# A recurrent attention kernel with a token-mixing layer: the written order of its instructions is replaced, and with it which engine copies, masks and sums

## The chip, the cores and the metric

One core of a Trainium2 chip runs the kernel. The time is device microseconds of one execution; a kernel's time is the median of its runs. The engines are TensorE (PE in the profile, its weight loads PEld), VectorE (DVE), ScalarE (ACT) and GpSimd (POOL); SyncE (SP) issues DMAs. GpSimd issues some DMAs too.

## What is computed

Six float32 inputs r, k, v, w, a, b of shape (4, 8, 768, 40) go through a recurrence over 768 steps for each of 4 batches and 8 heads, and its output, laid out as x of shape (4, 768, 320), goes through a mixing layer with four weight matrices. The output is float32 (4, 768, 320).

```python
for t in range(S):                       # state: (B, H, 40, 40)
    y[:, :, t] = einsum('bhd,bhde->bhe', rt, state)
    Sa = einsum('bhde,bhe->bhd', state, at)
    state_decay = state * wt[:, :, None, :] - einsum('bhd,bhe->bhde', Sa, bt)
    state = state_decay + einsum('bhd,bhe->bhde', vt, kt)
...
theta = x @ w_theta
zr = x * cos(theta)
zi = x * sin(theta)
y = w_tok_r @ zr + w_tok_i @ zi          # over the 768 tokens of a batch
u = x + y
out = u + maximum(u @ w_ch, 0)
```

## The kernel before, in words

Time is cut into chunks of 128 steps: 4 batches of 6 chunks make 24 tiles, numbered 0 to 23. A tile holds 128 steps of all 8 heads (128 partitions by 320 elements).

Within a tile the recurrence becomes matrix products. The logarithms of w (LN) are summed along the steps by two triangular products on TensorE: CSI, up to and with the step, and CSE, up to the step before, with five small products behind it for the decay over the whole tile. Exponentials of the sums (INVW, WI) scale k, b (KH, BH) and a (AH). The scaled inputs and r, v, cast to bf16 (CR, CV), are transposed on TensorE (TRK, TRA, TRR) and copied out of PSUM (EKBT, EAT, ERVT). Four sets of scores follow, each 8 products of 128 by 128: PSI and PHI (k and b against a), LV (v against r) and LU (the solved vectors nu against r). Each set fills two PSUM banks (tiles `sc`). Only entries above the diagonal count, so in the kernel before VectorE multiplies each set by a triangle of ones while it copies it to SBUF (`masked`, lines 374 to 379; EPSI, EPHI, ELV, ELU). Then X0, NU and NUT solve for nu, GT carries the state to the next tile (within a batch), GD transposes the state, and Y and EX give x.

The mixing layer works per tile too: XT, EXT, TH, ETH give theta; SIN gives cosine and sine of several tiles at once (`sines`, lines 483 to 489: three tiles together, for the last batch three, two and one); ZR and ZI multiply by x. YR sums twelve products (6 token blocks, real and imaginary) per tile, 24 tiles by 6 entries; EU adds x; UT, EUT, CH, EO, ST end the tile. The products need the two token matrices transposed: twelve row loads (LDT), twelve sets of transposes (WT) and copies (EWT).

The order of all this is written out by hand in the string `ORDER` (from line 19). An entry such as `EPSI:3V` names an operation, its tile, for some a part, its engine (A ScalarE, V VectorE, G GpSimd), and behind @ its PSUM tile (0 to 3 for the four one-bank tiles `sm`, 0 and 1 for the two-bank tiles `sc`). The loop at the end reads the entries one by one, so each engine runs its instructions in this order; the framework adds the waits for data and for buffers.

Loads are entries too: LDW, LDK, LDB, LDA, LDR, LDV load one input of one tile each (160 KB, `load`, line 282, on SyncE's queue; four buffers per input), ST stores from the same queue, LDT and LDC load matrices from GpSimd's queue (`row_load`, line 531). A load stands in line behind the loads ahead of it in the order.

Helpers record most instructions, so in the profile their lines stand for many operations: 259 is any product by `times`, 254 a copy on ScalarE, 256 a copy on another engine, 262 a product on TensorE, 266 a transpose, 525 the last step (EO), 487 a sine, 285 a load, 529 a store.

Of the kernel before, what the change touches and what calls it, by code (L numbers as in the profile page):

```python
# [19 lines left out]
LDK:0 LDW:1 LN:1A LDR:1 LDT:0.0G LDW:0 LN:0A LDC:0.2G LDB:0 LDC:0.0G LDA:0 LDV:1 LDW:2 CR:1A  # L20
LDR:0 LDT:1.0G CSE:1@0 LDV:0 LDC:0.3G LDW:3 WI:1A CSE:0@1 LDC:0.1G LDT:0.1G CSI:0@2 INVW:0A
LDA:1 WI:0A CSI:1@3 BH:0V LDB:3 KH:0V TRK:0@0 EKBT:0V INVW:1A CV:1A LDB:1 AH:0V TRA:0@2 EAT:0A
LDK:1 LN:2A PSI:0@0 PHI:0@1 EPSI:0V CSI:2@1 LDK:3 CR:0A EPHI:0V TRR:1@3 ERVT:1V CV:0A X0:0@0
LDK:2 ENX:0A LN:3A NU:0 LDR:2 TRR:0@2 ERVT:0A LV:1@0 LDB:2 CSE:2@3 LDA:2 ELV:1V AH:1V ENU:0A
INVW:2A LV:0@1 LDA:3 CSE:3@2 LDR:3 ELV:0V WI:3A TRA:1@0 EAT:1A GT:0@1 CSI:3@2 INVW:3A BH:1V
WI:2A LDV:2 KH:1V LDW:4 NUT:0@0 BH:3G EGT:0V TRK:1@2 EKBT:1V ENUT:0A LDV:3 KH:3G PSI:1@0 PHI:1@1
LDK:4 EPSI:1V KH:2G LDA:4 BH:2G X0:1@3 LDV:4 EPHI:1V AH:2G ENX:1A TRK:2@0 LU:0@0 TRA:2@1 LDR:4
EKBT:2V EAT:2A NU:1 LDR:5 CR:2G AH:3G TRK:3@2 ENU:1A PHI:2@1 GT:1@0 LDB:4 ELU:0V CV:2G EPHI:2V
EGT:1V NUT:1@1 CR:3G PSI:2@0 LDB:5 TRR:2@3 ENUT:1A LN:4A LDK:5 EPSI:2V ERVT:2A CV:3G TRA:3@1
EAT:3A LDW:5 LU:1@1 Y:0@0 X0:2@3 ENX:2A EKBT:3V LDW:6 CSE:4@1 LV:2@0 GD:0@2 EX:0V EGD:0A TRR:3@0  # L30
ELU:1V NU:2 CV:4G WI:4A LDW:7 CSI:4@2 INVW:4A PSI:3@1 AH:4G CR:4G LDA:5 Y:1@1 ENU:2A ERVT:3A
ELV:2V EPSI:3V NUT:2@2 PHI:3@0 KH:4G TRR:4@3 LDB:6 ENUT:2A ERVT:4A BH:4G LDK:6 GT:2@0 EX:1V
EPHI:3V LU:2@1 TRA:4@2 EGT:2V LDA:6 CR:5G EAT:4A XT:1@1 EXT:1A TRK:4@3 X0:3@2 LDV:5 ENX:3A LDV:6
TH:1@0 LN:5A ELU:2V LV:3@0 LDR:7 GD:1@1 NU:3 EKBT:4V ETH:1A ENU:3A CSI:5@3 INVW:5A ELV:3V LDV:7
PSI:4@1 BH:5G NUT:3@0 EGD:1A EPSI:4V GT:3@2 KH:5G XT:0@3 ENUT:3A LN:6A Y:2@1 LDK:7 CSE:5@0 LDR:6
EGT:3V EXT:0A PHI:4@0 WI:5A AH:5G EX:2V CSI:6@3 INVW:6A KH:6G X0:4@2 EPHI:4V LDB:7 LN:7A ENX:4A
LU:3@1 LDW:9 XT:2@0 EXT:2A TRK:5@1 CSE:6@3 ELU:3V NU:4 TH:2@0 WI:6A EKBT:5V ETH:2A BH:6G LV:4@0
ELV:4V TH:0@3 ENU:4A LDR:8 TRA:5@0 LDW:8 ETH:0A EAT:5A GD:2@1 CV:5G TRK:6@2 CV:7G PSI:5@1
NUT:4@3 EKBT:6V GT:4@0 LDA:8 EPSI:5V SIN:0.0A PHI:5@0 LDA:7 TRR:5@2 EGT:4V CV:6G AH:6G EGD:2V
X0:5@0 LDW:10 Y:3@1 ERVT:5V ENUT:4A ENX:5A EPHI:5V ZR:1G TRA:6@2 GD:3@3 EAT:6A LU:4@1 CR:7G  # L40
ZR:2G EX:3V EGD:3A NU:5 CR:6G CSE:7@1 ZR:0G ELU:4V LV:5@0 WI:7A LDB:9 CSI:7@2 INVW:7A LDB:8
LDV:10 TRR:6@3 LDR:10 ELV:5V ZI:1G LDK:8 PSI:6@1 BH:7G EPSI:6V Y:4@1 ENU:5A ERVT:6A PHI:6@0
LDK:9 LN:8A TRR:7@2 EX:4V X0:6@0 EPHI:6V ENX:6A LDR:9 NUT:5@3 ENUT:5A KH:7G TRK:7@1 EKBT:7V
LV:6@1 ERVT:7A CR:8G LDV:8 NU:6 ENU:6A GD:4@3 EGD:4A LDT:1.1G LU:5@0 CSI:8@1 AH:7G LDA:9 TRA:7@2
XT:3@0 ELV:6V NUT:6@3 EAT:7A ENUT:6A ELU:5V INVW:8A PSI:7@1 ZI:0G EXT:3V LN:9A GT:6@2 CSE:8@3
EPSI:7V TH:3@1 WI:8A LDR:11 Y:5@0 LN:10A AH:8G BH:8G LDV:9 EGT:6V XT:4@3 LDB:10 EX:5V PHI:7@0
ETH:3A LV:7@1 X0:7@1 EXT:4A EPHI:7V TRA:8@2 ENX:7A XT:5@3 TH:4@0 KH:8G EXT:5A LDW:12 EAT:8A
ZI:2G NU:7 LDK:10 TRK:8@3 CR:9G CR:10G ELV:7V CSI:9@2 ENU:7A INVW:9A BH:9G LU:6@0 TH:5@1 EKBT:8V
ETH:4A LDA:10 CSE:9@2 ETH:5A LDV:11 GT:7@3 ELU:6V CV:10G WI:9A LDB:12 PSI:8@1 EGT:7V Y:6@0
WT:0.0@1 EPSI:8V CV:8G NUT:7@2 LDW:11 PHI:8@0 WT:1.0@3 SIN:0.1A AH:9G EWT:0.0V TRR:8@1 ENUT:7V  # L50
LDT:2.0G EX:6V LDK:11 LU:7@1 EWT:1.0V EPHI:8V LDA:11 X0:8@2 ERVT:8A KH:9G WT:1.1@0 WT:0.1@3
ENX:8A EWT:0.1V CV:9G TRR:9@1 LDB:11 LV:8@0 ERVT:9A EWT:1.1V ZR:4G ZI:5G TRA:9@3 EAT:9A LDR:13
NU:8 LDV:14 ENU:8A LDA:12 ELV:8V TRK:9@0 XT:6@1 CSE:10@3 EKBT:9V GD:7@2 ZI:3G EXT:6V GD:6@0
ELU:7V ZR:3G CSI:10@1 INVW:10A LDT:4.0G PSI:9@0 LDV:12 EGD:7A EPSI:9V BH:10G EGD:6A PHI:9@1
LN:11A KH:10G GT:8@1 LDK:12 NUT:8@2 LDR:12 ENUT:8A EGT:8V EPHI:9V Y:7@0 X0:9@1 LDW:13 TH:6@2
WI:10A LU:8@0 ENX:9A EX:7V NU:9 ETH:6A ELU:8V LN:12A TRK:10@3 ENU:9A XT:7@2 LV:9@1 LDT:2.1G
AH:10G EXT:7A TRA:10@0 EKBT:10V ZI:4G Y:8@1 EAT:10A ELV:9V TH:7@2 ETH:7A ZR:5G LDK:13 GD:8@3
EGD:8A NUT:9@0 CR:11G EX:8V PSI:10@0 CV:11G GT:9@2 LDR:15 ENUT:9V CSI:11@3 INVW:11A EPSI:10V
XT:8@1 TRR:10@0 EXT:8A LDT:3.0G PHI:10@1 EGT:9V LDR:14 ERVT:10A CSE:11@3 WT:2.0@1 LDA:13
EPHI:10V LDV:13 KH:11G X0:10@2 WI:11A LDB:13 BH:11G ENX:10A TRR:11@0 LV:10@0 EWT:2.0V ERVT:11A  # L60
LU:9@1 AH:11G LDT:3.1G YR:0.0@3 ELV:10V NU:10 ENU:10A YR:0.1 TRK:11@1 ELU:9V LDW:14 TRA:11@0
LDT:5.0G LDT:4.1G YR:0.2 EAT:11A YR:0.3 YR:0.4 YR:0.5 EKBT:11V CSI:12@2 INVW:12A EU:0V TH:8@0
ETH:8A LN:13A PSI:11@0 EPSI:11V PHI:11@1 UT:0@1 CSE:12@2 CR:12G EUT:0A LDW:15 LDB:14 NUT:10@3
GT:10@0 ENUT:10A WI:12A EPHI:11V Y:9@1 CV:12G WT:3.0@3 KH:12G LV:11@0 AH:12G EGT:10V LU:10@1
EX:9V CR:15G WT:2.1@2 WT:3.1@0 SIN:1.0A YR:1.0@1 EWT:3.0V EWT:2.1V YR:1.1 BH:12G GD:9@3 EWT:3.1V
X0:11@2 YR:1.2 ELU:10V LDK:14 XT:9@0 YR:1.3 ENX:11A YR:1.4 EGD:9A ELV:11V NU:11 ENU:11A YR:1.5
ZI:8G EXT:9A TRA:12@3 TRK:12@2 Y:10@0 EU:1V EAT:12A EKBT:12V WT:4.0@3 LDT:5.1G NUT:11@1 ZR:6G
EX:10V CSI:13@2 INVW:13A KH:13G PSI:12@1 EWT:4.0V PHI:12@0 EPSI:12V ENUT:11A TRR:12@0 CH:0@3
EO:0V ERVT:12A ZR:7G GD:10@2 YR:2.0@1 YR:2.1 EGD:10A EPHI:12V ST:0 CSE:13@3 BH:13G X0:12@0
ENX:12A LU:11@1 LDA:14 WI:13A YR:2.2 ZI:6G ELU:11V UT:1@2 CR:13G LDR:17 LN:14A LV:12@0 EUT:1A  # L70
XT:10@3 CV:13G ELV:12V YR:2.3 NU:12 ENU:12A Y:11@2 EXT:10A AH:13G LDB:15 YR:2.4 LN:15A TRR:13@0
EX:11V TRA:13@3 ERVT:13V YR:2.5 EAT:13A ZI:7G CV:14G TRK:13@2 CR:14G EU:2V TH:9@0 EKBT:13V
GT:12@3 EGT:12V ETH:9A CH:1@1 PSI:13@1 PHI:13@0 EO:1V EPSI:13V ST:1 LDW:16 EPHI:13V CSI:14@2
INVW:14A KH:14G NUT:12@0 ENUT:12A CSE:14@3 WI:14A LDK:15 LDR:18 YR:3.0@1 TH:10@2 YR:3.1 LDA:16
X0:13@0 LDV:16 ETH:10A XT:11@3 EXT:11V LDA:15 CSI:15@2 ENX:13A LDB:16 AH:14G LV:13@1 LU:12@0
INVW:15A BH:14G TRA:14@3 NU:13 ENU:13A YR:3.2 ELV:13V ELU:12V YR:3.3 YR:3.4 YR:3.5 EU:3V EAT:14A
LDV:15 TH:11@2 ETH:11A KH:15G TRK:14@0 CSE:15@3 EKBT:14V LN:16A LDW:20 GT:13@2 EGT:13V WI:15A
WT:4.1@1 LDK:17 LDK:16 NUT:13@0 WT:5.1@3 EWT:4.1V ZR:8G WT:5.0@2 EWT:5.1V YR:4.0@1 LDW:17
SIN:1.1A EWT:5.0V PSI:14@1 PHI:14@0 LDV:17 AH:15G TRR:14@3 Y:12@2 EPSI:14V ENUT:13A EX:12V
ZR:11G BH:15G EPHI:14V YR:4.1 YR:4.2 YR:4.3 ERVT:14A YR:4.4 ZI:10G UT:2@2 EUT:2V YR:4.5 LU:13@1  # L80
X0:14@0 EU:4V ELU:13V GD:12@3 ENX:14A CH:2@2 EGD:12A EO:2V XT:12@1 EXT:12A CV:15G LV:14@0 ST:2
UT:3@3 NU:14 ZR:9G TRA:15@1 EUT:3A ENU:14A TRK:15@2 LDR:16 TH:12@3 EAT:15A ELV:14V EKBT:15V
CH:3@0 EO:3V LDA:18 ETH:12A ZI:9G TRR:15@1 CSI:16@3 INVW:16A ERVT:15V PSI:15@1 EPSI:15V ST:3
PHI:15@0 BH:16G ZR:10G YR:5.0@2 LDA:17 NUT:14@0 LDV:18 ENUT:14A CSE:16@1 YR:5.1 GT:14@3 GD:13@0
WI:16A Y:13@1 EPHI:15V KH:16G LN:17A LDW:21 CV:17G LDW:18 EGT:14V CR:18G LU:14@1 LV:15@0 EGD:13A
YR:5.2 LDK:19 EX:13V CR:17G X0:15@0 ELU:14V AH:16G YR:5.3 ENX:15A LDW:19 CV:16G YR:5.4 LDB:17
XT:13@3 EXT:13A YR:5.5 TRK:16@1 EU:5V LDR:19 NU:15 ENU:15A CSE:17@3 TH:13@2 EKBT:16V CR:16G
TRA:16@0 Y:14@1 ETH:13A ELV:15V LDB:20 ZI:11G EAT:16A LDV:19 TRR:16@2 EX:14V LDK:18 PSI:16@1
EPSI:16V WI:17A AH:17G PHI:16@0 LN:18A NUT:15@0 ENUT:15A CV:18G XT:14@3 YR:6.0@1 YR:6.1 EPHI:16V
EXT:14A YR:6.2 CR:19G ERVT:16A YR:6.3 TH:14@0 UT:4@3 LDA:20 LU:15@1 EUT:4V ELU:15V LV:16@0  # L90
CSI:17@2 GT:15@3 LDB:18 ETH:14A INVW:17A LN:19A CH:4@0 UT:5@2 YR:6.4 EGT:15V EUT:5A YR:6.5 EO:4V
# [541 lines left out]
```

## Time and profile before

| | us |
|---|---|
| median of 3 runs (lowest, highest) | 225.95 (224.32, 226.55) |
| the profiled execution, its own time | 228.5 |
| its span, first to last instruction | 226.7 |
| TensorE busy | 199.1 |
| VectorE busy | 189.4 |
| ScalarE busy | 150.9 |
| GpSimd busy | 118.1 |

The busy time of TensorE is that of its matrix products, whose ends are modelled; where products follow each other closely their spans overlap, so the rate is read from one start to the next. On the other engines too an instruction's span reaches a little over the start of the next. A timeline row gives the start, the span, the engine, the line, the operation with its tiles and shape, how many were merged, and in brackets how long the engine had been idle and what ended it. Row groups give the number, the sum and the mean.

### The profile page before, as it was taken

How to read it: one execution, taken by the hardware profiler on the slowest of the kernel's cores; microseconds unless marked ns; L12 is line 12 of the kernel's file. 1: busy time of each engine (PE TensorE's matmuls, PEld its weight loads, DVE VectorE, ACT ScalarE, POOL GpSimd, SP SyncE). 2: the span in 40 equal slices, each digit the busy share in tenths (PEclk: the TensorE clock that was granted, in tenths of full speed). 3: DMA queues.
4: the chain of work that ended last, by engine and by line, in shares of the span. 5: the costliest groups of instructions: out<-in, count | busy, mean ns of one | idle time of the engine just before them, and what ended most of it. 6: DMA issues, size and time to landing. Idle time of an engine off the chain costs nothing.

```text
span 226.7 us, 8000 instructions
## 1 busy us (share of the span) xinstructions
PE 199.1 (88%) x3344; PEld 158.1 (70%) x3344; DVE 189.4 (84%) x298; ACT 150.9 (67%) x293; POOL 118.1 (52%) x181
## 2 busy tenths in 40 slices
...
GB/s 104 195 192 184 156 181 136 166 176 168 143 181 160 166 189 164 188 151 190 104 159 156 195 157 161 186 172 181 159 162 32 4 61 1 61 42 48 29 90 87
DMA packets 155684, 30.81 MB, mean 136 GB/s; under 512 B 150400, under 2 KB 155648, under 8 KB 155648
## 3 DMA queue, kind: packets, MB, share of 16 engines
q1 hardware_dynamic: 153216, 27.54, 66.7%
q0 software_dynamic: 2432, 2.77, 7.9%
q8 instruction: 26, 0.43, 0.8%
q14 instruction: 10, 0.08, 0.1%
...
## 4 chain that ended last, share of the span: by engine, by line
PE 50%; issue 6%; DMA 5%; POOL 4%; DVE 4%; ACT 2%; POOLq 0%; DVEq 0%; ACTq 0%
PE sm L262 28%; PE sm L266 13%; PE sc L262 9%; DMA raw_w<-in_w_dram 5%; POOL kb L259 2%; DVE psi L259 1%; POOL rv L256 1%; ACT rvT L254 1%; POOL zi L259 1%; POOL zr L259 1%; DVE phi L259 1%; DVE lamv L259 0%; DVE lamu L259 0%; POOL ah L259 0%; DVE oo L525 0%
## 5 line engine op out<-in xcount | busy, mean ns | idle before, releaser
L259 POOL TENSOR_TENSOR kb<-raw_b,invW 128x320 bf16<-128x320 f32 x22 | 19.0, 863 | 33.2 <-DVE kb L259 20.1
L262 PE MATMUL sm<-zr,wtok_r 128*128 128x320 bf16 x120 | 34.2, 300 | 0.0
L262 PE MATMUL sm<-zi,wtok_i 128*128 128x320 bf16 x120 | 34.2, 299 | 0.0
L259 DVE TENSOR_TENSOR psi<-sc,mask_p 128x1024 bf16<-128x1024 f32 x24 | 29.2, 1219 | 3.4 <-PE sc L262 3.3
L259 DVE TENSOR_TENSOR lamu<-sc,mask_p 128x1024 bf16<-128x1024 f32 x24 | 29.2, 1218 | 1.4 <-PE sc L262 1.3
L259 DVE TENSOR_TENSOR lamv<-sc,mask_p 128x1024 bf16<-128x1024 f32 x24 | 29.2, 1217 | 1.4 <-PE sc L262 1.3
L259 POOL TENSOR_TENSOR ah<-raw_a,Wi 128x320 bf16<-128x320 f32 x22 | 19.0, 864 | 21.4 <-issue 8.7
L259 DVE TENSOR_TENSOR phi<-sc,mask_p 128x1024 bf16<-128x1024 f32 x24 | 29.2, 1216 | 0.9 <-PE sc L262 0.9
L259 POOL TENSOR_TENSOR zi<-cs,x 128x320 bf16<-128x320 f32 x24 | 19.0, 798 | 10.1 <-ACT cs L487 10.1
L259 POOL TENSOR_TENSOR kb<-raw_k,invW 128x320 bf16<-128x320 f32 x22 | 18.9, 862 | 7.8 <-ACT invW L302 5.9
L259 POOL TENSOR_TENSOR zr<-cs,x 128x320 bf16<-128x320 f32 x21 | 16.6, 793 | 7.9 <-ACT cs L487 7.9
L291 ACT ACTIVATE lw<-raw_w 128x320 bf16<-128x320 f32 x24 | 11.4, 473 | 12.7 <-DMA raw_w<-in_w_dram 12.7
L262 PE MATMUL sc<-aT,kbT 64*128 64x128 bf16 x384 | 17.5, 227 | 2.4 <-ACT aT L359 1.0
L256 DVE COPY kbT<-sm 128x1024 bf16<-128x1024 bf16 x24 | 16.5, 686 | 3.8 <-PE sm L266 3.7
L266 PE MATMUL sm<-ident,kb 128*128 128x128 bf16 x192 | 16.5, 235 | 2.2 <-DVE kb L259 1.2
L359 ACT ACTIVATE aT<-sm 128x512 bf16<-128x512 bf16 x24 | 14.5, 603 | 5.5 <-PE sm L266 5.2
L262 PE MATMUL sm<-lw,mask_p 128*128 128x320 bf16 x24 | 7.8, 323 | 11.7 <-ACT lw L291 11.6
L254 ACT COPY rvT<-sm 128x1024 bf16<-128x1024 bf16 x16 | 16.3, 1018 | 2.2 <-PE sm L266 2.2
L266 PE MATMUL sm<-ident,rv 128*128 128x128 bf16 x192 | 15.7, 227 | 1.8 <-POOL rv L256 1.7
L254 ACT CAST nx<-sm 128x320 bf16<-128x320 f32 x24 | 10.2, 424 | 10.7 <-PE sm L262 10.6
L262 PEld LDWEIGHTS <-wtok_i 128*128 128x128 bf16 x144 | 14.0, 97 | 4.2 <-issue 0.8
L262 PEld LDWEIGHTS <-wtok_r 128*128 128x128 bf16 x144 | 14.0, 97 | 4.1
...
## 6 DMA issues: line engine op xcount, KB each, us to landing
...
```

Of the source, the lines that this page charges most:

```text
L254: keep(nc.scalar.copy(out=out, in_=in_))
L256: keep(eng[e].tensor_copy(out=out, in_=in_))
L259: keep(eng[e].tensor_tensor(out=out, in0=in0, in1=in1, op=ALU.mult))
L262: keep(nc.tensor.matmul(out, lhsT=lhsT, rhs=rhs, start=start, stop=stop, skip_group_check=True))
L266: keep(nc.tensor.transpose(out=out, in_=in_, identity=ident))
L291: keep(nc.scalar.activation(out=q.lw[:, :, 0:D], in_=q.raw_w, func=AF.Ln))
L359: keep(nc.scalar.mul(out=q.aT, in_=q.aps[:, 0:512], mul=-1.0))
```

## The change

The string ORDER is another one, with all entries newly placed and partly on other engines, and these functions change:

- A score set may be copied out of PSUM by ScalarE without the mask (EPSI, EPHI, ELV, ELU with A). A new entry (MPSI, MPHI, MLV, MLU) then lets GpSimd zero the entries below the diagonal in SBUF, in place.
- CSI may be an addition on VectorE (of CSE's result and the logarithms) instead of a product on TensorE; INVW then takes exp of the negative.
- For some tiles the old state is added to the new one by VectorE (EGA) instead of by a product with the identity in GT.
- The last tile of a batch leaves out the five small products of CSE, whose result is not used there.
- Sines are taken for one tile at a time, into a buffer of each chunk's own (six `cs` tiles instead of one for three chunks).
- FILL products of a zeroed tile `warm` (128 by 512) with itself, into PSUM tiles that stand free, 17 entries, all within the entries of the first tiles.

How many entries stand on which engine (A, V, G; T is TensorE), where that differs:

| entries | before | after |
|---|---|---|
| scores copied (EPSI, EPHI, ELV, ELU) | V 96 | V 45, A 51 |
| masks by GpSimd | 0 | G 51 |
| KH, BH, AH | G 66, V 6 | G 46, V 26 |
| CR, CV | G 44, A 4 | G 36, A 12 |
| CSI | T 24 | T 9, V 15 |
| EGA | 0 | V 10 |
| ERVT | A 16, V 8 | A 5, V 19 |
| EKBT | V 24 | V 22, A 2 |
| ENUT | A 20, V 4 | A 5, V 19 |
| ENX, ENU, ETH | A 72 | A 48, V 24 |
| EGD | A 17, V 3 | A 7, V 13 |
| EXT, EUT | A 36, V 12 | A 17, V 31 |
| EWT | V 12 | V 7, A 5 |
| ZR, ZI | G 45, V 3 | G 38, V 10 |
| SIN | 9 (two instructions each) | 24 (two each) |

The scores on VectorE by tiles: of the 32 sets of tiles 2 to 9, 32 before and 19 after; of the 32 of tiles 10 to 17, 32 and 13; of the 24 of tiles 18 to 23, 24 and 8. EGA stands for tiles 9, 10, 13 to 16 and 19 to 22, CSI on VectorE for tile 9 and all later ones. Also for tiles 2 to 9, before and after on VectorE: ERVT 1 and 8, KH and BH 0 and 7, ENX, ENU and ETH 0 and 7, ENUT 2 and 4, EGD 1 and 4, EUT 3 and 6, EXT 2 and 4, CSI and EGA 0 and 2, ZR and ZI 0 and 2, EKBT 8 and 7; EWT 12 and 7 in all.

How the loads stand: PSI of tile 0, 1, 2, 3, 4, 5 has 15, 25, 31, 36, 44, 50 input loads ahead of it before, and 8, 16, 22, 27, 33, 42 after; PSI of tile 16 has 120 and 110. Row loads (LDT) ahead of PSI of tile 1: 3 before, 6 after. Behind the last input load stand 89 of the 144 YR entries before (last load LDB:21) and 72 after (LDR:23). Behind GpSimd's last entry stand 27 and 24 of them. Each order has 13 changes of ScalarE's table behind the first load of it.

The first lines of ORDER after:

```
LDK:0 LDW:0 LDB:0 LDC:0.2G LDA:0 LDT:1.0G LDV:0 LDT:2.1G LN:0A FILL:6.4@4 FILL:3.1@4 CSI:0@0
LDW:1 LDT:1.1G LDT:0.0G CSE:0@3 INVW:0A LDC:0.3G WI:0A LDR:0 KH:0G LDT:2.0G LDT:0.1G BH:0V
FILL:14.1@4 TRK:0@2 EKBT:0A LDC:0.0G LDC:0.1G AH:0V LDB:1 FILL:22.1@4 TRA:0@1 EAT:0A FILL:10.1@5
PHI:0@0 PSI:0@1 EPHI:0A EPSI:0V CV:0A LDA:1 MPHI:0G FILL:19.1@3 X0:0@0 ENX:0A FILL:7.1@3 NU:0
ENU:0V FILL:7.1@2 NUT:0@3 GT:0@2 EGT:0V LDK:1 ENUT:0V LN:1A FILL:7.1@4 CSE:1@1 CSI:1@0 CR:0A
```

`FILL:6.4` is six products of 4 times 128 columns, `FILL:14.1` fourteen of 128. All FILL entries together are 168 times 128 columns.

The core of the diff below the order:

```diff
+    warm = consts.tile([128, 512], BF16, name="warm")
+    nc.vector.memset(warm, 0.0)
...
-    cs = mw.tile([128, 2, 3, DM], FP32, name="cs")
+    cs = [mw.tile([128, 2, DM], FP32, name=f"cs_{n}") for n in range(NCH)]
...
-    def csi(i, b):
+    def csi(i, e, b):
         q = tiles[i]
+        if e:
+            q.csum = tile_of(sml, [128, H, D], FP32, "csum")
+            keep(eng[e].tensor_tensor(
+                out=q.csum, in0=q.cse[:, 0:DM].rearrange("p (h d) -> p h d", h=H),
+                in1=q.lw[:, :, 0:D], op=ALU.add))
+            return
         q.csi = bank(b)
...
+        if hasattr(q, "csum"):
+            keep(nc.scalar.activation(out=q.invW, in_=q.csum, func=AF.Exp, scale=-1.0))
+            return
...
         mm(q.cse[:, 0:DM], tri_exc, q.lw[:, :, 0:D], True, True)
+        if is_last(i):
+            return
...
         P = getattr(tiles[i], src)
+        if e == "A":
+            copy(e, s.rearrange("p a b c -> p (a b) c"), P.rearrange("p a b c -> p (a b) c"))
+            return
         times(e, s.rearrange("p a b c -> p (a b) c"), P.rearrange("p a b c -> p (a b) c"),
               mask_p.to_broadcast([128, 2 * G, 128]))
+
+    def mask(i, name):
+        flat = getattr(tiles[i], name).rearrange("p a b c -> p (a b) c")
+        keep(nc.gpsimd.affine_select(
+            out=flat, in_=flat, compare_op=ALU.is_ge, fill=0.0, base=-1,
+            pattern=[[0, 2 * G], [1, 128]], channel_multiplier=-1))
...
-        first = is_first(i)
+        first = is_first(i) or i in added
...
+    def add_gt(i, e):
+        q = tiles[i]
+        q.gsum = tile_of(sml, [128, 8, D], FP32, "gsum")
+        keep(eng[e].tensor_tensor(
+            out=q.gsum, in0=q.gps[:, 0:DM].rearrange("p (n d) -> p n d", d=D),
+            in1=gt_t[(i + 1) % 2].rearrange("p g c d -> p (g c) d")[:, :, 0:D], op=ALU.add))
...
-    def sines(bi, n):
-        js = parts[bi][n]
+    def sines(i):
         table[0] = None
         for c in range(2):
             keep(nc.scalar.activation(
-                out=cs[:, c, 0:len(js)], in_=th[:, js[0]:js[-1] + 1], func=AF.Sin,
+                out=cs[i % NCH][:, c], in_=th[:, i % NCH], func=AF.Sin,
                 bias=(pi2_col[:, :], 0.0)[c]))
...
+    def fill(n, cols, b):
+        pt = banks(b - 4)[:, 0] if b > 3 else bank(b)
+        flat = pt.rearrange("p a b -> p (a b)") if b > 3 else pt
+        for _ in range(n):
+            mm(flat[:, 0:128 * cols], warm[:, 0:128], warm[:, 0:128 * cols], True, True)
```

263 lines of the change are left out of this document (136 added, 127 removed).

## The prediction

> **What bounds the kernel now.** First the page: share of each engine, the chain, the loads.
>
> ```profile
> span 226.7 us, 8000 instructions
> PE 199.1 (88%) x3344; PEld 158.1 (70%) x3344; DVE 189.4 (84%) x298; ACT 150.9 (67%) x293; POOL 118.1 (52%) x181
> PE 50%; issue 6%; DMA 5%; POOL 4%; DVE 4%; ACT 2%; POOLq 0%; DVEq 0%; ACTq 0%
> q0 software_dynamic: 2432, 2.77, 7.9%
> ```
>
> TensorE has the most work and half of the chain, but an average hides stages. So, second, the busy times by stretches, cut where the rate of TensorE changes (35, below) and where the loads end (168).
>
> ```profile
> core 0: us, PE busy (x) PEld busy (x) DVE busy (x) ACT busy (x) POOL busy (x), PEclk, DMA share, GB/s
> 0.00:35.00 35.00, 18.02 (x205) 13.43 (x206) 17.86 (x57) 12.23 (x26) 12.78 (x28) 1.00 1.04 169
> 18.00:35.00 17.00, 14.71 (x179) 11.32 (x179) 12.16 (x15) 7.07 (x16) 6.99 (x11) 1.00 1.07 174
> 35.00:85.00 50.00, 46.76 (x946) 37.65 (x944) 48.89 (x63) 44.45 (x87) 33.51 (x50) 1.00 0.98 165
> 85.00:139.00 54.00, 52.95 (x959) 43.25 (x958) 51.68 (x71) 41.54 (x81) 34.86 (x53) 1.00 0.91 161
> 139.00:168.00 29.00, 28.16 (x512) 22.68 (x509) 27.54 (x39) 22.50 (x46) 15.47 (x21) 1.00 0.94 171
> 168.00:227.00 59.00, 53.17 (x737) 41.11 (x735) 43.44 (x72) 30.16 (x56) 21.52 (x30) 0.99 0.16 51
> ```
>
> Four stages are to be seen. Up to 35 us no engine is full; TensorE does 205 of its 3344 products there, and 179 of them between 18 and 35. From 35 to 85 VectorE is full (48.89 of 50). From 85 TensorE is full (52.95 of 54, 28.16 of 29), VectorE close behind. Behind the last load only TensorE counts. The DMA engines are busy from 0 to 168 at a share of about one. Third, why 179 products need 17 us: TensorE's timeline.
>
> ```profile
> 28.41 1.03 PE L262 MATMUL sc<-aT,kbT 64*128 64x128 bf16 x16 [0.79 <-DVE kbT L256]
> 30.82 1.02 PE L266 MATMUL sm<-ident,kb 128*128 128x128 bf16 x8
> 31.78 0.61 PE L262 MATMUL sc<-rvT,nuT 64*128 64x128 bf16 x8
> 43.20 0.61 PE L266 MATMUL sm<-ident,kb 128*128 128x128 bf16 x8
> 46.54 0.30 PE L262 MATMUL sm<-gt,ident 128*128 128x320 bf16 x1
> 46.68 0.20 PE L262 MATMUL sm<-rv,kb 128*128 128x80 bf16 x1
> 47.81 0.17 PE L262 MATMUL sm<-off_diag,ident 128*128 128x8 bf16 x1
> 48.01 0.40 PE L262 MATMUL sc<-aT,kbT 64*128 64x128 bf16 x8
> 48.34 0.31 PE L262 MATMUL sm<-lw,ntri_inc 128*128 128x320 bf16 x1
> 48.49 0.20 PE L262 MATMUL sm<-gt,aT 128*128 128x80 bf16 x1
> ```
>
> Eight transposes take 0.96 us from start to start at 30.82, and a span of 1.02 against 0.61 at 43.20; the last one's passage of about 0.2 (as at 46.68) taken off, 0.82 against 0.41. So early products run at half rate, though the column PEclk says 1.00: it shows another throttle.
>
> **The change part by part. The start.** TensorE's 14.71 us between 18 and 35 at full rate would be 7.4: up to 7.3 saved, if nothing else sets the pace. The loads may:
>
> ```profile
> 0.74 0.43 SPq L285 DMA_DIRECT2D raw_k<-in_k_dram  x1
> 166.57 0.58 SPq L285 DMA_DIRECT2D raw_b<-in_b_dram  x1
> 4.82 0.47 ACT L291 ACTIVATE lw<-raw_w 128x320 bf16<-128x320 f32 x1 [2.81 <-DMA raw_w<-in_w_dram]
> 18.68 1.22 DVE L259 TENSOR_TENSOR psi<-sc,mask_p 128x1024 bf16<-128x1024 f32 x1 [2.07 <-PE sc L262]
> ```
>
> 144 loads in 165.8 us are one per 1.16 us. PSI of tiles 0 to 5 stood behind 15, 25, 31, 36, 44, 50 loads and now stands behind 8, 16, 22, 27, 33, 42: some 9 fewer, 10.4 us. Against it, three more row loads go early: q0 moved 16 DMAs in 7.9% of 226.7, 1.1 us each, so 3.4; 7.0 stay. Clock and loads are two limits of one stretch, not two gains. I take -6; the ends are -10 (loads alone, LDT hidden) and +2. That end is the FILL: 168 blocks of 128 columns at 0.96/8 = 0.12 us are 20 us at half rate, and TensorE is idle 35 - 18.02 = 17 us there. At full rate (half of that) 10 us fit into the gaps. What hides FILL is that idle time; where a gap is too short, the score products behind it wait.
>
> The Trainium skill (TensorE: Matmul & The Clock Gate, Part 1) says that about 3.4 us of sustained activity double the clock and an idle window halves it; the late release at 35 in this trace, with gaps of 0.79 us before, fits, and by that rule the FILL would bring all 7.3, a total of 217.
>
> **35 to 85: VectorE.**
>
> ```profile
> L256 DVE COPY kbT<-sm 128x1024 bf16<-128x1024 bf16 x24 | 16.5, 686 | 3.8 <-PE sm L266 3.7
> L254 ACT COPY rvT<-sm 128x1024 bf16<-128x1024 bf16 x16 | 16.3, 1018 | 2.2 <-PE sm L266 2.2
> L254 ACT CAST nx<-sm 128x320 bf16<-128x320 f32 x24 | 10.2, 424 | 10.7 <-PE sm L262 10.6
> L259 DVE TENSOR_TENSOR gt<-sm,Wi 128x320 bf16<-128x320 f32 x20 | 9.7, 484 | 0.1
> L256 DVE COPY uT<-sm 128x384 bf16<-128x384 bf16 x8 | 2.8, 351 | 1.1 <-PE sm L266 1.1
> L487 ACT ACTIVATE cs<-th,pi_col 128x960 f32<-128x960 f32 x7 | 7.7, 1096 | 0.1
> L487 ACT ACTIVATE cs<-th,pi_col 128x320 f32<-128x320 f32 x1 | 0.6, 561 | 0.0
> 67.28 1.22 DVE L259 TENSOR_TENSOR phi<-sc,mask_p 128x1024 bf16<-128x1024 f32 x1
> 68.42 1.22 DVE L259 TENSOR_TENSOR lamv<-sc,mask_p 128x1024 bf16<-128x1024 f32 x1
> ```
>
> This stretch is about tiles 2 to 9. Off VectorE go 13 score sets, 13 x 1.22 = 15.9, one EKBT 0.7 and about four EWT, 2.0 by the EKBT row's rate. Onto it come 7 ERVT x 0.686 = 4.8; 7 KH and BH, 2 Z, CSI and EGA, 11 x 0.484 = 5.3 (the state's product, same shape); 7 casts ENX, ENU, ETH at between 0.351 (the row for 384 bf16) and 0.484, near the second since they read float32: 3.2; 10 short copies (ENUT, EGD, EUT, EXT) at some 0.36, 3.6. Together -1.7; starts follow each other 0.08 closer than spans (67.28 to 68.42 for 1.22), and there are 17 more instructions: -3.1. The relief is small: what VectorE gives up in scores it takes back in copies.
>
> And ScalarE steps into its place. It gets 13 sets at 1.018 (the nearest copy of that size), one EKBT, 5 casts of r and v at 0.424 and four EWT at some 0.8 by its rate: 19.6. It gives up 7 ERVT, 7.1, and 17 short copies at some 0.45, 7.7. Sines one by one cost 3 x 0.561 - 1.096 = 0.6 more per instruction of three tiles, two to a set, two sets in this stretch: 2.4. So 44.45 + 7.2 = 51.7, over VectorE's 45.8. Not all of it need fall here, since sines can wait. The stretch's bound, 48.89, changes from one engine to the other. I take -1; the ends are -3 (VectorE alone) and +3 (ScalarE alone).
>
> **From 85: TensorE.** A CSI product takes 0.15 from start to start (48.34 to 48.49), the state's 0.14 (46.54 to 46.68), the five small ones of CSE 0.20 (47.81 to 48.01): 15 x 0.15 + 10 x 0.14 + 4 x 0.20 = 4.5, all at tile 5 or later, where TensorE is full. But VectorE stands at 51.68 of 54 up to 139, and there gets 8 CSI and 5 EGA at 0.484 (6.3) beside copies, for 19 sets given up. So I take -3, ends -4.5 and 0. At the end both engines have less.
>
> **GpSimd's masks and the shared path.**
>
> ```profile
> masks.py:66 POOL TENSOR_SCALAR_AFFINE_SELECT mask_p<-mask_p 128x128 bf16<-128x128 bf16 x1 | 0.3, 287 | 0.0
> L256 POOL CAST rv<-raw_r 128x320 bf16<-128x320 f32 x22 | 9.8, 450 | 5.7 <-DMA raw_r<-in_r_dram 5.1 <-PE sm L266 0.6
> L259 POOL TENSOR_TENSOR kb<-raw_b,invW 128x320 bf16<-128x320 f32 x22 | 19.0, 863 | 33.2 <-DVE kb L259 20.1
> L259 DVE TENSOR_TENSOR zr<-cs,x 128x320 bf16<-128x320 f32 x3 | 1.7, 588 | 0.0
> 211.54 0.79 POOL L259 TENSOR_TENSOR zi<-cs,x 128x320 bf16<-128x320 f32 x1 [1.51 <-ACT cs L487]
> 211.88 0.80 DVE L259 TENSOR_TENSOR zr<-cs,x 128x320 bf16<-128x320 f32 x1
> ```
>
> A select of 1024 elements isn't in the trace. From one of 128 at 0.287 and a cast of 320 at 0.450: 0.85 ns per element more, 1.05 us. The cast scaled without any floor: 1.44. Eight pieces of 0.24 (a select of 0.287 less the overlap) 1.9. I take 1.3, since it has one input and one output like the cast. 51 x 1.3 = 66. Off GpSimd go 20 x 0.863, 8 x 0.450 and 7 x 0.79 = 26.4: 118.1 - 26.4 + 66 = 158, under TensorE. A mask sits between a score's copy and its use, and KH, BH, AH of later tiles queue behind it; what hides that is that scores are made a tile or so ahead.
>
> Shared path: zr started 0.34 behind zi at 211.54 and took 0.80, not 0.484: 0.31 of wait for zi's rest. Such two-input products from SBUF on VectorE go from 9 to 36. With GpSimd busy 158/219 = 0.72: 27 x 0.72 x 0.31 = 6 of delay, half of it beside other waits. With ScalarE's, VectorE's and GpSimd's queues now all close to full, I add +2; ends 0 and +12 (below).
>
> **Sum.** -6 - 1 - 3 + 2 = -8 on the span of 226.7: 218.7. The profiled execution took 228.5, the median is 225.95; the same -8 on the median gives 218.
>
> **Rivals.** *GpSimd becomes the bound (slower).* At 1.9 a mask, GpSimd has 118.1 - 26.4 + 97 = 189 us. It begins at about 7 (KH of tile 0 follows the first logarithm, at 4.82, its sum and an exponential), and at 90% busy needs 210. Before, zi at 211.54 was its last instruction and 27 YR groups took the 14.4 us behind it; now 24 do, 13: 7 + 210 + 13 = 230. It decides from 1.7 a mask on (7 + 178/0.9 + 13 = 218). For it speaks the row at 0.24 a piece, against it the cast's rate.
>
> *The shared path costs in full.* If VectorE waits for half a mask, 0.65, at 27 x 0.72 places, that is 12.6, where VectorE is the bound or next to it: 218 - 2 + 12.6 = 228.6 at most, 226 where a part is beside other waits: no change. For it speaks the zr of 0.80, against it the mean of all three zr, 0.588, by which the other two took 0.48. The Trainium skill (SBUF — State Buffer, Who interferes with whom) states it as a rule: a VectorE instruction with two SBUF inputs and a GpSimd one that reads SBUF exclude each other for their whole length; by it every such meeting costs.
>
> *The FILL doesn't bring the full rate early, or overruns its gaps.* Start +2 instead of -6, loads notwithstanding: 226, or 223 where only the gain is lost. For it: 20 us of FILL against 17 us of gaps. Against: fewer loads ahead.
>
> *All goes well:* -10 - 3 - 4.5 and 0 give 208.
>
> **How the numbers follow.** The forecast, 212 to 222: 0.50. All well, below 212: 0.15. FILL fails, 222 to 226: 0.09, a third of it under the 1% line of 223.7 (1% is about what a measurement of this kernel can tell from no change). Shared path, 224 to 228: 0.09. GpSimd bound, above 228.2: 0.17. So faster 0.50 + 0.15 + 0.03 = 0.68, same 0.06 + 0.09 = 0.15, slower 0.17. The range from 207 to 229 leaves out some 0.04 below and 0.15 above.
>
> **What would show it.** Start: eight transposes at 0.61 by 20 us, and the first score mask before 15 us (18.68 before); wrong if the spans stay at 1.02 up to 30. VectorE: 45 score rows left, its busy share in the second stretch still above 90%. Masks: mean of the select; above 1.7 the forecast falls. Shared path: mean of kb and zr on VectorE against 0.484; at 0.8 and more the third rival holds. TensorE: idle gaps with GpSimd's select as releaser in the stretch behind 85 would make the prediction wrong.

## The result, and the profile after

The changed kernel takes 235.54 us (median of 4 runs, 234.81 to 237.38), the kernel before 226.25 (4 runs, 224.32 to 227.21): a ratio of 1.0434, 95% interval 1.0342 to 1.0526. It is slower; 218 was forecast, with a range up to 229. Below, a ratio compares a run with the kernel before on the same chip (median 226 to 230 us there) and leaves out executions over 1.5% above the fastest of the same kernel.

The page of the changed kernel: span, engines, shares of the chain of waits.

```profile
span 233.9 us, 8304 instructions
PE 209.9 (90%) x3449; PEld 166.0 (71%) x3449; DVE 196.7 (84%) x372; ACT 172.4 (74%) x310; POOL 154.4 (66%) x197
PE 43%; DVE 27%; DMA 10%; ACT 9%; issue 4%; POOL 3%; SPq 2%; DVEq 0%; ACTq 0%
```

VectorE's share of the chain went from 4% to 27%, although its busy time rose by only 7.3 us (189.4 to 196.7). GpSimd, with 36 us more, has 3%: it isn't the bound. Four of the prediction's stretches, in the changed kernel:

```profile
core 0: us, PE busy (x) PEld busy (x) DVE busy (x) ACT busy (x) POOL busy (x), PEclk, DMA share, GB/s
18.00:35.00 17.00, 15.62 (x274) 13.21 (x272) 11.55 (x18) 11.98 (x25) 6.33 (x7) 0.92 0.99 167
35.00:85.00 50.00, 47.47 (x951) 38.25 (x949) 48.41 (x78) 47.10 (x91) 40.45 (x53) 1.00 0.97 165
85.00:139.00 54.00, 46.75 (x772) 36.84 (x769) 50.15 (x83) 42.15 (x72) 39.27 (x50) 0.94 0.81 139
168.00:234.00 66.00, 60.52 (x860) 46.53 (x857) 53.03 (x104) 39.65 (x71) 36.49 (x43) 0.99 0.36 81
```

The loss is in the third: from 85 to 139 TensorE is busy 46.75 instead of 52.95, at a granted clock of 0.94. Something stopped it there. VectorE's timeline at that place, then GpSimd's, then TensorE's:

```profile
94.25 0.49 DVE L461 TENSOR_TENSOR gsum<-sm,gt 128x320 f32<-128x320 f32 x1 [0.22 <-PE sm L272]
94.78 4.97 DVE L269 TENSOR_TENSOR gt<-gsum,Wi 128x320 bf16<-128x320 f32 x1
99.68 0.48 DVE L562 SCALAR_TENSOR_TENSOR oo<-sm,u 128x320 f32<-128x320 f32 x1
```

```profile
94.27 0.59 POOL L570 DMA_DIRECT2D wtok_row<-in_moe_w_tok_r_dram  x1
94.88 1.10 POOL L411 TENSOR_SCALAR_AFFINE_SELECT lamv<-lamv 128x1024 bf16<-128x1024 bf16 x1
95.91 0.46 POOL L266 CAST rv<-raw_v 128x320 bf16<-128x320 f32 x1
96.31 0.45 POOL L266 CAST rv<-raw_r 128x320 bf16<-128x320 f32 x1
96.70 0.55 POOL L570 DMA_DIRECT2D wtok_row<-in_moe_w_tok_i_dram  x1
97.26 1.10 POOL L411 TENSOR_SCALAR_AFFINE_SELECT lamu<-lamu 128x1024 bf16<-128x1024 bf16 x1
98.30 1.10 POOL L411 TENSOR_SCALAR_AFFINE_SELECT lamv<-lamv 128x1024 bf16<-128x1024 bf16 x1
99.34 0.72 POOL L266 CAST rv<-raw_r 128x320 bf16<-128x320 f32 x1
```

```profile
99.81 0.25 PE L272 MATMUL sm<-gt,aT 128*128 128x80 bf16 x1 [4.18 <-DVE gt L269]
100.59 0.47 PE L272 MATMUL sm<-zi,wtok_i 128*128 128x320 bf16 x1
103.73 1.02 PE L276 MATMUL sm<-ident,rv 128*128 128x128 bf16 x8
107.07 0.40 PE L276 MATMUL sm<-ident,nu 128*128 128x128 bf16 x4
```

The state's product of tile 10 (EGT, `gt`) takes 4.97 us where it took 0.48. Its data were there: the instruction had begun. Seven GpSimd instructions ran in that time, each at its ordinary length but the last one, 0.72. TensorE, which needs the new state, sat idle for 4.18, and then ran at half rate: a product of 320 columns took 0.47 (0.30 at full rate), eight transposes 1.02, until about 106.

By groups, VectorE's products in the changed kernel (line 269 is `times`):

```profile
L269 DVE TENSOR_TENSOR gt<-gsum,Wi 128x320 bf16<-128x320 f32 x10 | 13.7, 1373 | 0.2
L269 DVE TENSOR_TENSOR gt<-sm,Wi 128x320 bf16<-128x320 f32 x10 | 4.8, 479 | 1.2 <-PE sm L272 1.2
L269 DVE TENSOR_TENSOR kb<-raw_b,invW 128x320 bf16<-128x320 f32 x10 | 7.5, 753 | 2.2 <-DMA raw_b<-in_b_dram 2.1
L269 DVE TENSOR_TENSOR kb<-raw_k,invW 128x320 bf16<-128x320 f32 x10 | 6.9, 687 | 0.1
L269 DVE TENSOR_TENSOR zr<-cs,x 128x320 bf16<-128x320 f32 x4 | 3.9, 977 | 0.0
```

The first two rows are the same operation of the same size. With its input in PSUM (`sm`) it takes 0.479; with the sum in SBUF (`gsum`, the new entry EGA) it has two SBUF inputs and takes 1.373 on average. The whole surplus over 0.484 of such products, these groups with 6 ah at 0.609 and 6 zi at 0.672, is 8.9 + 2.7 + 2.0 + 2.0 + 0.8 + 1.1 = 17.5 us.

### The profile page after: what moved, and what is told of

It is laid out like the page before. It is cut to its first block, busy times and chain, and to the rows that moved or that the text cites. A ratio compares the mean times of both kernels' runs of the same rounds, so it can differ in the third digit from the quotient of the medians.

```text
span 233.9 us, 8304 instructions
## 1 busy us (share of the span) xinstructions
PE 209.9 (90%) x3449; PEld 166.0 (71%) x3449; DVE 196.7 (84%) x372; ACT 172.4 (74%) x310; POOL 154.4 (66%) x197
## 4 chain that ended last, share of the span: by engine, by line
PE 43%; DVE 27%; DMA 10%; ACT 9%; issue 4%; POOL 3%; SPq 2%; DVEq 0%; ACTq 0%
PE sm L272 22%; PE sm L276 13%; PE sc L272 9%; DMA raw_v<-in_v_dram 5%; DVE gt L269 5%; DVE kb L269 3%; SPq L298 2%; DVE phi L269 2%; DVE psi L269 2%; DMA raw_k<-in_k_dram 2%; ACT cs L525 2%; DVE lamv L269 1%; DVE rvT L266 1%; DMA raw_w<-in_w_dram 1%; DVE lamu L269 1%
## 5 line engine op out<-in xcount | busy, mean ns | idle before, releaser
L411 POOL TENSOR_SCALAR_AFFINE_SELECT lamv<-lamv 128x1024 bf16<-128x1024 bf16 x18 | 20.4, 1133 | 8.3 <-ACT lamv L264 6.5
L269 POOL TENSOR_TENSOR kb<-raw_b,invW 128x320 bf16<-128x320 f32 x14 | 12.6, 898 | 11.3 <-ACT invW L324 10.1
L269 DVE TENSOR_TENSOR psi<-sc,mask_p 128x1024 bf16<-128x1024 f32 x14 | 17.0, 1217 | 3.0 <-PE sc L272 3.0
L264 ACT CAST lamv<-sc 128x1024 bf16<-128x1024 f32 x18 | 18.4, 1022 | 0.8 <-PE sc L272 0.4
L411 POOL TENSOR_SCALAR_AFFINE_SELECT psi<-psi 128x1024 bf16<-128x1024 bf16 x10 | 11.2, 1116 | 9.7 <-ACT psi L264 8.9
L411 POOL TENSOR_SCALAR_AFFINE_SELECT phi<-phi 128x1024 bf16<-128x1024 bf16 x11 | 12.5, 1137 | 6.2 <-ACT phi L264 6.2
L411 POOL TENSOR_SCALAR_AFFINE_SELECT lamu<-lamu 128x1024 bf16<-128x1024 bf16 x12 | 13.1, 1095 | 4.9 <-ACT lamu L264 4.8
L276 PEld LDWEIGHTS <-kb 128*128 128x128 bf16 x192 | 12.0, 99 | 5.5 <-DVE kb L269 2.5
L269 DVE TENSOR_TENSOR phi<-sc,mask_p 128x1024 bf16<-128x1024 f32 x13 | 15.8, 1214 | 0.1
L272 PEld LDWEIGHTS <-rvT 64*128 64x128 bf16 (+1 forms) x272 | 13.7, 95 | 2.4 <-ACT rvT L264 0.9
```

The source lines that it names most:

```text
L264: keep(nc.scalar.copy(out=out, in_=in_))
L269: keep(eng[e].tensor_tensor(out=out, in0=in0, in1=in1, op=ALU.mult))
L272: keep(nc.tensor.matmul(out, lhsT=lhsT, rhs=rhs, start=start, stop=stop, skip_group_check=True))
L276: keep(nc.tensor.transpose(out=out, in_=in_, identity=ident))
L411: keep(nc.gpsimd.affine_select(out=flat, in_=flat, compare_op=ALU.is_ge, fill=0.0, base=-1, pattern=[[0, 2 * G], [1, 128]], channel_multip ...
```

## The experiments

**The state's sum taken out, or kept in PSUM.** Both move the product of tile 15 ahead of the transpose of tile 13's state, which thus reads a later state; that part of the result differs.

```diff
  e1: - EGA:9V ... EGA:22V      (EGT in their places, the identity product back)
  e2: - q.gsum = tile_of(sml, [128, 8, D], FP32, "gsum")
      + q.gsum = q.gps[:, 0:DM].rearrange("p (n d) -> p n d", d=D)
                                (each EGT right behind its EGA)
```

> The state is again added by the product with the identity for all tiles; EGT stands where EGA stood and reads PSUM. Theory (VectorE's EGT with both inputs in SBUF was kept from its second operand by GpSimd's queue; once for 4.5 us, which also let TensorE fall to half rate for some 6 us): EGT back to 0.48 at all 20 places, no gap of TensorE near 95 us, about 7.5 us for that place and some of the other 8 us of VectorE's time: 225 us (222 to 228). Rival (the new order is too full on VectorE, ScalarE and GpSimd, and the long EGT only stands where a wait would be anyway): 232 or more.

> EGA stays on VectorE, but writes its sum over GT's result in PSUM, so that EGT has one input in SBUF again; EGT stands right behind EGA. Theory (it is the second SBUF input that waits for GpSimd, not the extra addition): EGT at 0.48 everywhere, 227 us (224 to 230), some 2 us above the kernel without EGA. Rival (the addition on VectorE, in the chain from tile to tile, costs by itself): 232 to 236, and the kernel without EGA well below it.

Measured: 1.0043 (0.9997 to 1.0089) without the sums, 0.9989 (0.9951 to 1.0028) with them in PSUM. In the second every state product took 0.48 to 0.49. VectorE still does every addition there; only where the sum lies differs. So the loss hangs on the second SBUF input of these ten products. The addition by itself costs nothing to be seen in this order: the run that keeps it is not above the one without it, where 2 us had been expected. But without the second SBUF input the new order is no more than level with the old.

The run without the sums shows such a wait at another product of two SBUF inputs, a zr; VectorE's row, then the DMA issue ahead of it on GpSimd, then TensorE, which waits for VectorE's next copy:

```profile
122.84 2.89 DVE L264 TENSOR_TENSOR zr<-cs,x 128x320 bf16<-128x320 f32 x1
122.15 0.59 POOL L565 DMA_DIRECT2D wtok_row<-in_moe_w_tok_r_dram  x1
126.39 0.49 PE L271 MATMUL sm<-ident,wtok_row 128*128 128x128 bf16 x6 [2.12 <-DVE kbT L261]
```

**The same, with the reference's result.** The transpose of tile 13's state goes ahead of the sum of tile 15.

> All ten sums in PSUM, as in the run with the sums in PSUM, but with the transpose of the state of tile 13 moved ahead of the sum of tile 15, so that the reference's result is computed in full. Both theories expect the same as that run had: a ratio of 0.995 to 1.003.

1.0031 (0.9992 to 1.0069): level. This kernel is the base of the later ones.

**No FILL.**

```diff
- FILL:6.4@4 FILL:3.1@4 ... FILL:1.1@3      (all entries)
```

> All FILL entries out. If they bring the full rate of TensorE early: half rate up to 30 us or more, and 238 to 240. If loads set the start anyway, or FILL costs what it gives: 234 to 236. If FILL holds up the first tiles: 232.

1.0366 (1.0295 to 1.0436), not to be told from the changed kernel. The transposes of r, first in the changed kernel, then without FILL:

```profile
21.26 0.61 PE L276 MATMUL sm<-ident,rv 128*128 128x128 bf16 x8
```

```profile
20.60 1.01 PE L270 MATMUL sm<-ident,rv 128*128 128x128 bf16 x8
23.65 1.06 PE L270 MATMUL sm<-ident,kb 128*128 128x128 bf16 x8
29.98 0.62 PE L270 MATMUL sm<-ident,rv 128*128 128x128 bf16 x8
```

FILL does bring the full rate, some 8 us earlier, and hardly any time: tile 3's state product comes at 43.75 with it and at 44.20 without. The start waits for something else. The product of tile 10 takes 4.98 us in this run, so that wait is no accident of one execution.

**What the two engines do to each other, alone.** A small kernel (nothing of the reference is computed) gives VectorE eight products in each of its stages, beside a run of one kind of GpSimd instruction.

> Leaves out the whole computation: VectorE does eight products of 128 by 320 float32 in each of six phases, with GpSimd idle but for one cast (phase 0), with 8 selects of 1024 (1), 18 casts of 320 (2), 8 selects but VectorE's one input in PSUM (3), 10 two-input products (4), selects, casts and memsets in turn (5). Theory: 0.48 each in phases 0 and 3; in phases 1, 2, 4 one product of VectorE waits for more than one GpSimd instruction, up to the whole row of them. Rival (each waits for at most the instruction that runs): at most 1.1 more per product, in turn with GpSimd's.

Products with two SBUF inputs beside selects, then the same with one input in PSUM:

```profile
12.91 7.57 POOL L56 TENSOR_SCALAR_AFFINE_SELECT big<-big 128x1024 bf16<-128x1024 bf16 x6
13.10 5.26 DVE L61 TENSOR_TENSOR do<-gate,xb 128x320 bf16<-128x320 f32 x4
31.99 3.27 DVE L64 TENSOR_TENSOR do<-pa,gate 128x320 bf16<-128x320 f32 x8 [5.55 <-ACT gate L74]
```

1.3 each (5.26/4) beside selects at the same spacing (7.57/6 = 1.26), against 0.41 each (3.27/8) with one input in PSUM. The two engines take turns, one instruction each, as the rival said: a wait of a whole select is 0.9, and 4.97 isn't reached. Taking turns alone does not explain tile 10.

**The row loads near tile 10 issued later.** The two DMA issues among GpSimd's rows above move behind a later mask.

```diff
- ... WT:3.1@1 LDT:3.0G TRK:12@3 ... EXT:8V LDT:4.1G EPSI:12V ... MLV:10G
+ ... WT:3.1@1 TRK:12@3 ... EXT:8V EPSI:12V ... MLV:10G LDT:3.0G LDT:4.1G
```

> The new kernel with two entries moved: the row loads LDT:3.0 and LDT:4.1, which GpSimd issued ahead of and within the row of instructions that kept EGT of tile 10 waiting for 4.5 us, stand behind MLV:10. Theory A (a wait of that length needs GpSimd's issue of a DMA, after which its instructions follow each other without a gap for VectorE): EGT of tile 10 at 1.5 or less, TensorE not idle and at full rate there, 228 us (226 to 230). Theory B (any full queue of GpSimd does it): EGT of tile 10 still 3 us or more, 233 to 236.

1.014 (1.0065 to 1.0215), and the product of tile 10:

```profile
96.70 1.28 DVE L264 TENSOR_TENSOR gt<-gsum,Wi 128x320 bf16<-128x320 f32 x1
```

The wait falls to that of one turn. So the wait at tile 10 needs both: a second SBUF input (with the sum in PSUM the product takes 0.49, also where this is the only edit, below), and the DMAs issued by GpSimd beside it.

**DMA issues against memsets, alone.** The small kernel again (nothing of the reference is computed): GpSimd's row of selects and casts holds two DMA issues in stages 0 to 3, memsets in their places in stages 4 to 7; VectorE does four state products beside it.

> Leaves out the whole computation. In eight phases GpSimd has a row of instructions as it had beside EGT of tile 10: in phases 0 to 3 DMA issue, select, cast, cast, DMA issue, select, cast, cast, select, select, cast, cast; in phases 4 to 7 a memset of 768 columns in place of each DMA issue. VectorE first does 1, 2, 3 or 4 products from PSUM, so that its first product from two SBUF inputs (in EGT's form) meets another place of the row. Theory A: in phases 0 to 3 one of them takes 3 us or more, in phases 4 to 7 none over 1.5. Theory B (the place in the row decides): long ones in both groups. If none is over 1.5 in either, the wait of 4.5 us needs something that these rows lack.

Four products each: three stages with DMA issues, then two with memsets (the longest and the shortest of each kind, and one between):

```profile
4.49 4.17 DVE L72 TENSOR_TENSOR gt<-gate,wi 128x320 bf16<-128x320 f32 x4
15.70 6.83 DVE L72 TENSOR_TENSOR gt<-gate,wi 128x320 bf16<-128x320 f32 x4
38.91 6.03 DVE L72 TENSOR_TENSOR gt<-gate,wi 128x320 bf16<-128x320 f32 x4
71.14 3.24 DVE L72 TENSOR_TENSOR gt<-gate,wi 128x320 bf16<-128x320 f32 x4
82.22 2.84 DVE L72 TENSOR_TENSOR gt<-gate,wi 128x320 bf16<-128x320 f32 x4
```

1.04 to 1.71 each against 0.71 to 0.81. The longest single one beside a DMA issue took 2.15, a select and a cast passing ahead of it; beside memsets 1.41. The effect is there, but at half of tile 10's size: the 3 us of theory A are not reached, so these rows lack a part of what makes 4.97.

**Tile 10 alone.** The changed kernel, with the sum of this one tile in PSUM:

```diff
+ q.gsum = (q.gps[:, 0:DM].rearrange("p (n d) -> p n d", d=D) if i == 10
+           else tile_of(sml, [128, 8, D], FP32, "gsum"))
```

> The changed kernel with one instruction altered: the state sum of tile 10 alone is written in place in PSUM, so that the product behind it has one input from SBUF. Theory (the place at tile 10 is the largest single loss of the shared path): the state's product of tile 10 falls from 4.97 us to about 0.5, TensorE keeps its full rate behind it, and the ratio to the kernel before goes from 1.043 to 1.010 to 1.020. Rival (the loads issued by GpSimd only need some product with two SBUF inputs beside them): another such product of the same stretch stretches in its place, and the ratio stays at 1.030 or more.

1.0102 (1.0036 to 1.0167). The row, with the DMA issue 0.5 us ahead of it as before:

```profile
95.11 0.59 POOL L571 DMA_DIRECT2D wtok_row<-in_moe_w_tok_r_dram  x1
95.63 0.49 DVE L269 TENSOR_TENSOR gt<-sm,Wi 128x320 bf16<-128x320 f32 x1
```

One instruction's operand moved, and 3.3 of the 4.3 per cent are gone.

**More products to GpSimd.** The base kernel, with 33 of VectorE's two-input products (KH, BH, AH, ZR, ZI from tile 2 on) given to GpSimd.

> EGA writes its sum in PSUM as in the experiment before (with GD of tile 13 moved ahead of EGT of tile 15, so that it reads the state it should), and the 33 products of tiles 2 and later that VectorE makes from two SBUF inputs (KH, BH, AH, ZR, ZI) go to GpSimd at the same places of the order. Theory (waits for GpSimd on VectorE are the rest of what the new order loses): VectorE gives up some 25 us, GpSimd gets 28 and stands near 180 of 222: 222 us (218 to 226). Rival (GpSimd then is the bound, and transposes wait for its products): 232 to 240, with TensorE's idle time before TRK and TRA released by GpSimd.

1.0316 (1.02 to 1.0432). The rival held: VectorE fell to 169.1 us, GpSimd rose to 173.1, and TensorE waits for it:

```profile
L272 PE MATMUL sm<-ident,kb 128*128 128x128 bf16 x192 | 16.2, 224 | 9.4 <-POOL kb L265 9.1 <-DVE gt L265 0.3
```

**The sums in the old order.** The kernel before, with EGA at the ten tiles and nothing else.

> One part alone on the kernel before: EGA on VectorE with its sum in SBUF, for the same ten tiles, right ahead of EGT. Theory (the second SBUF input is what costs): VectorE gets 4.8 us of additions and EGT of these tiles takes 0.8 to 1.3, more where GpSimd is full: 230 to 234 against 226. Rival (in an order with more room on GpSimd it is hidden): 226 to 228.

1.0108 (1.0028 to 1.0188): the ten additions with their sums in SBUF cost some 1% even without the masks. That lies between the two forecasts. EGT of these tiles takes 0.635 on average, not 0.8 to 1.3, so here the waits are the smaller part; how much the additions and how much the waits cost was not separated in this order.

**No masks.** The base kernel without the 51 masks; ScalarE's copies multiply by zero, so these scores' values are left out too.

```diff
- MPHI:0G MLU:0G ... MPHI:23G MLU:23G      (all M entries)
- copy(e, s..., P...)
+ nc.scalar.mul(out=s..., in_=P..., mul=0.0)
```

> The kernel with all ten sums in PSUM, without the 51 masks on GpSimd; ScalarE's copies of the same scores multiply by zero instead, so that the later arithmetic stays in range. This leaves the masking of 51 score sets and their values out. GpSimd falls from 152 us to about 96. Theory (what is left of the loss is VectorE's and GpSimd's turns and the way of a score through two engines): the products KH, BH, AH, ZR and ZI on VectorE fall to 0.5 us each, some 9 us of VectorE's work go, and the ratio falls to 0.965 to 0.985. Rival (ScalarE with 172 us and the chain through its copies set the pace, or TensorE itself): 0.988 to 1.002.

0.9862 (0.9804 to 0.9919), 1.7% under the base. VectorE's busy time is 184.2 (base 188.3), GpSimd's 95.5. The theory is borne out in part: VectorE gives up 4.1 us instead of 9, since KH, BH, ZR and ZI still take 0.58 to 0.67 (AH 0.485), and the ratio ends just above its range.

**Three early row loads moved back.** The base kernel, with halves of rows 1 and 2 issued behind the masks of tiles 4, 6 and 8; the first line of ORDER loses one, the second two.

```diff
- ... LDV:0 LDT:2.1G LN:0A ... LDW:1 LDT:1.1G LDT:0.0G ... KH:0G LDT:2.0G LDT:0.1G
+ ... MLV:4G LDT:1.1G ... MLV:6G LDT:2.1G ... MLV:8G LDT:2.0G
```

> The kernel with all ten sums in PSUM, and the three row loads that the new order issues early (halves of rows 1 and 2) moved back behind the masks of tiles 4, 6 and 8. Theory (the start is paced by the loads, the three row loads cost 3.7 us there): the first masks of tiles 1 to 5 come 2 to 3.7 us earlier, and the time falls by 2 to 3.5 us against all sums in PSUM: a ratio of 0.983 to 0.992 to the kernel before. Rival (from 85 us on VectorE sets the pace, and an earlier start only waits longer there): the start gains, the milestones behind 110 us do not, ratio 0.995 to 1.002.

0.986 (0.9805 to 0.9915). The profiled execution took 229.78 us, the others 224.1 to 226.0, and it shows tile 10's wait at another place:

```profile
108.95 0.59 POOL L566 DMA_DIRECT2D wtok_row<-in_moe_w_tok_i_dram  x1
110.69 3.33 DVE L265 TENSOR_TENSOR kb<-raw_b,invW 128x320 bf16<-128x320 f32 x1
```

The same kernel was run again, and another with that load too moved behind the next product on GpSimd (`LDT:5.1G` behind `KH:14G`):

> The kernel with the sums in PSUM and three early row loads moved back, once more, unchanged, for a profile of an execution with the time that its others have. In the first profile (229.78 us, where the others took 224.1 to 226.0) the lead of 3.4 us at tile 1 was gone by tile 6, and a product of tile 14 on VectorE waited until 114.0. Theory (the start is paced by the loads and its lead is kept): the state's product of tile 6 comes some 2 to 3 us before the 65.25 of the kernel with the sums in PSUM, and so do the later ones. Rival (the lead is eaten between tiles 1 and 6 in every execution, by an engine that is full there): tile 6 at 65 again, and the gain of 1.7% comes from behind it.

> The same with one more load moved: the row load that GpSimd issues just ahead of the product of tile 14 that waited in the first profile goes behind the next product on GpSimd. Theory (a load issued by GpSimd lets several of its instructions pass ahead of a waiting product of VectorE, wherever it stands): that product stays under 1.4 us in every execution, and the times keep to the lower group, 224 to 226 us, a ratio of 0.980 to 0.990. Rival (the wait of tile 14 has another cause, the loads' and engines' timing): it comes in some executions again, and the times scatter up to 230.

0.9931 (0.9892 to 0.997) when run again, 0.9917 (0.9873 to 0.9962) with the last load moved. Both compute the reference in full and are slightly faster than the kernel before, by about 0.7 and 0.8%. In these two profiles the product of tile 14 took 1.15 and 0.62. With the load in its place, ending 1.15 us ahead, this product took 1.15 or 1.16 in eight traces of the changed kernel and its variants with masks, and 3.33 in one. So the place depends on the timing of an execution, and the second run does not prove that moving the load was needed.

The lead of the start, by the state's product of tile 6: 61.86 in the first of the two, 65.17 in the second (base: 65.02, which the expectation gives as 65.25). In the second a load of r came late, TensorE idled 1.62 us up to 55.42, and its granted clock was 0.51 from 55 to 60. In the profile of 229.78 us the lead is gone at tile 6 as well (65.05). It is kept in some executions and lost in others. Where it is kept, tile 9's state product comes at 81.80 instead of the base's 84.48, and from there to the end both take 140.8.

## Why the prediction was wrong, point by point

The state's product of a tile is a good mark, since each tile needs the one before. Tiles 3 and 9 in the kernel before, then after:

```profile
47.60 0.48 DVE L259 TENSOR_TENSOR gt<-sm,Wi 128x320 bf16<-128x320 f32 x1
88.45 0.48 DVE L259 TENSOR_TENSOR gt<-sm,Wi 128x320 bf16<-128x320 f32 x1
```

```profile
43.75 0.48 DVE L269 TENSOR_TENSOR gt<-sm,Wi 128x320 bf16<-128x320 f32 x1
84.09 0.49 DVE L269 TENSOR_TENSOR gt<-gsum,Wi 128x320 bf16<-128x320 f32 x1
```

The same mark for tile 9 with tile 10's sum in PSUM, in the base kernel, and without masks:

```profile
84.94 0.49 DVE L269 TENSOR_TENSOR gt<-gsum,Wi 128x320 bf16<-128x320 f32 x1
```

```profile
84.48 0.49 DVE L265 TENSOR_TENSOR gt<-sm,Wi 128x320 bf16<-128x320 f32 x1
```

```profile
84.99 0.49 DVE L261 TENSOR_TENSOR gt<-sm,Wi 128x320 bf16<-128x320 f32 x1
```

From tile 9's mark to the end of the span (226.7, 233.9, 228.0, 225.3, 222.6) it is 138.3 us before, 149.8 after, 143.1 with tile 10's sum in PSUM, 140.8 in the base, 137.6 without masks.

- **Start, -6: right in sign, too large.** Tile 3 comes 3.9 earlier (47.60 to 43.75), and the first mask on VectorE stands at 12.26, within the 15 forecast. Of the two limits the prediction weighed, the loads held and the clock did not: FILL brought the full rate and hardly any time. That the three row loads cost 3.4 there was right: with them moved back tile 3's mark stands at 40.15 instead of the base's 43.49, 3.3 earlier. The count of loads saved, 10.4, was too much: 47.60 to 40.15 is 7.5. The sentence on the clock gate (the Trainium skill, TensorE: Matmul & The Clock Gate, Part 1) was borne out as a rule: full rate from 21 (forecast by 20) instead of 35, and half rate again when TensorE had been idle for 4.18 us. That the FILL would bring "all 7.3" by it was not, since the loads were the other limit. The rate was full once before, at 11.5, and was lost in a wait of 3.48 us for tile 0's v, a load. The prediction also read the column PEclk as that of another throttle. In the changed kernel the column stands at 0.50 from 18 to 20 and from 99.8 to 106, where products run at half rate, so it is the same one; what the column misses is the half rate before TensorE's first full rate.
- **35 to 85, -1: near in size, not in its mechanism.** From tile 3 to tile 9 it takes 40.9 before and 40.3 after. But the bound did not change from VectorE to ScalarE: VectorE stayed the fullest at 48.41 of 50, where 45.8 was forecast, and ScalarE rose to 47.10, not 51.7, since a part of its added work falls into other stretches.
- **From 85, -3: not seen.** TensorE was relieved, but it was no longer the bound: its only gap over 1 us from 85 to 139 (4.18 us) was ended by VectorE's state product, and none by a select of GpSimd. In the base, where no state product waits, the way from tile 9 to the end is 140.8 instead of 138.3: 2.5 longer. Without the masks it is 137.6, so the masks on GpSimd cost some 3.2 of it, by the products that still meet selects on VectorE and by the way of a score through two engines; how these two share it was not separated. The prediction had named VectorE as second in this stretch (51.68 of 54) and still let two thirds of TensorE's saving count.
- **GpSimd's masks: right.** The selects took 1.095 to 1.137 us by group (1.3 taken, 1.05 estimated), GpSimd's sum 154.4 (158). ScalarE's score copies took 1.009 to 1.022 (1.018). The rival in which GpSimd bounds the kernel gave 230, of all the rivals' times the nearest to the measured one, but that is luck: GpSimd has 3% of the chain. With 33 more products on GpSimd it came true (1.0316).
- **The shared path, +2, ends 0 and +12: the step that failed.** The wait per place was about right where it was counted: the 36 products other than the state's lost 8.6 us together, 0.24 each, against 0.72 x 0.31 = 0.22. But "two-input products from SBUF on VectorE go from 9 to 36" is wrong: it costs EGA as one more product of 0.484 and overlooks what it does to the EGT behind it, whose input goes from PSUM to SBUF. That makes 46, and the ten left out are the ones that every later tile waits for. And a wait was taken to be at most the rest of one GpSimd instruction, which tile 10 broke with 4.5 us. From tile 9 to the end, tile 10's place is worth 149.8 - 143.1 = 6.7 us (idle, then half rate), the other nine 143.1 - 140.8 = 2.3.
- **The rival "the shared path costs in full"** (the third, as the prediction's last part counts) had the right mechanism, and its mark held for zr (0.977, over 0.8) and not for kb (0.69 to 0.75). Its 224 to 228 was short since its places were the same 27. The rule beside it (the Trainium skill, SBUF — State Buffer, Who interferes with whom: the two instructions exclude each other for their whole length) agrees with the small kernel's turns of 1.3 us; the passing of several GpSimd instructions at tile 10 goes beyond it.

The sum as measured, up to tile 9 -4.4 and behind it +11.6 (tile 10's place 6.7, the other nine 2.3, the rest of the new order 2.5), gives the span's 7.2. Forecast were -7 and -1.
